# Strassen's seven products for the gate and up projections of five of seven feature groups

## The chip, the cores and the metric

The kernel runs on one core of a Trainium2 chip. A time is the device time of one execution in microseconds (us). Engines have the profile's short names: PE is TensorE's matmul, PEld its weight load, DVE is VectorE, ACT is ScalarE, POOL is GpSimd, SP is the queue that issues most DMAs. In the profile L321 is line 321 of the kernel before.

## What is computed

Two layers, each an attention step and a feed-forward step, with a residual. The change is in the feed-forward step alone:

```python
x = x + _A_ref(_layernorm(x), wq, wk, wv, wo)
x = x + (silu(n @ w_gate) * (n @ w_up)) @ w_down      # n = _layernorm(x)
# ... and both once more; x is 2048 rows of 448, w_gate and w_up are 448 x 1792
```

## The kernel before

**Precision.** Every float32 operand of a feed-forward product is held as a high and a low part in float32r (`split`, L139 and L140, on POOL for weights; ACT makes the high part and DVE the low part of activations). A product of two is then three matmuls: high by high, high by low, low by high.

**Tiles.** The 2048 rows are four chunks `c` of 512; the 1792 features are 14 slices `fc` of 128, in seven groups of two (`FG`). The 448 inputs are three full blocks `k` of 128 partitions and a rest of 64. Activations lie transposed, in `xh` and `xl` (`self.X[c]`).

**A unit** (`unit`) is one slice by one chunk. Its matmuls use half the array's rows each, and two of them run side by side (`side_by_side`, L321): one on partitions 0 to 63, one on 64 to 127, on two different PSUM banks. Two such matmuls are called a pair here. A unit has 21 pairs of 512 columns for gate and up (11, then 10 with the banks exchanged) and 12 pairs of 448 columns for down (6 and 6). On PE the order is: gate and up 11, the first down half of the unit before, gate and up 10, the second down half of the unit before. Between two halves ACT reads one column of each bank (`between`, L328, into `seen`), so that the second half waits until the first is complete. Behind gate and up come, for each unit: ACT silu (L888), DVE product (L889), ACT high part (L890), DVE low part (L893). The down product accumulates in four banks over both slices of a group, and then goes into `xres` (`accumulate`: two tiles on DVE, L792, two copied by ACT, L795, and added by POOL, L796).

**Order.** Nothing is rescheduled: each engine runs its instructions in the order in which the program issues them (`manual_schedule`). `pend` holds the down halves and adds of the last unit, `soon` and `mid` hold steps of the layer norm of chunk 3 that are given to certain units of group 0; `turned` transposes chunk 3 on PE in the middle of the unit of chunk 2, slice 1. A chunk's loop runs inside a group's. Weights of slice `fc + 3` are loaded and split by POOL at the last chunk of slice `fc` (`weights`); the raw weights have one buffer (`wr`).

Attention comes before and after. It owns `keys`, `qts`, `qraw` and `kd`, which are idle in the feed-forward step.

Of the kernel before, what the change touches and what calls it, by code (L numbers as in the profile page):

```python
# [8 lines left out]
F32 = mybir.dt.float32  # L9
F32R = mybir.dt.float32r  # L10
# [5 lines left out]
P = 128  # L16
S = 2048
# [35 lines left out]
def forward(  # L53
# [84 lines left out]
    def split(hi, lo, raw):  # L138
        nc.gpsimd.tensor_scalar(hi, raw, 1.0, 0.0, ALU.mult, ALU.add)  # L139
        nc.gpsimd.tensor_tensor(lo, raw, hi, ALU.subtract)  # L140
# [16 lines left out]
    def weights(fc):  # L157
        fs = slice(P * fc, P * fc + P)
        r = wpool.tile([P, 4, 2, P], F32, name="wr")
        for b, src in enumerate((w_gate, w_up)):  # L160
            rows3(r[:, :, b, :], src[:, fs])
        rd = wpool.tile([P, D], F32, name="wdr")
        nc.sync.dma_start(rd, w_down[fs, :])
# [114 lines left out]
    def flipped(tiles, k, pt, copy, steps=(0, 1)):  # L278

        xh, xl, xd = tiles  # L280
        twice = xd if k == 3 else None
        if 0 in steps and twice is None:
            copy(xh[:, k, :], pt)
        elif 0 in steps:
            copy(xh[0:64, k, :], pt[0:64, :])
            copy(xd[64:128, :], pt[64:128, :])
        if 1 in steps and k < 3:
            nc.vector.tensor_tensor(xl[:, k, :], pt, xh[:, k, :], ALU.subtract)
        elif 1 in steps:
            high = xh[64:128, k, :] if twice is None else xd[64:128, :]  # L290
            nc.vector.tensor_tensor(xh[64:128, k, :], pt[64:128, :], high, ALU.subtract)

    def product_T(po, a_h, a_l, tiles):

# [21 lines left out]
    def side_by_side(lower, upper):  # L316

        assert len(lower) == len(upper)
        for two in zip(lower, upper):
            for po, (a, b), start, stop in two:  # L320
                nc.tensor.matmul(po, a, b, start=start, stop=stop, skip_group_check=True)  # L321
# [3 lines left out]
    def between(*pos):  # L325

        for i, po in enumerate(pos):
            nc.scalar.copy(seen[:, i : i + 1], po[:, 0:1])  # L328
# [416 lines left out]
                        ff.left.pop(0)()  # L745

    groups = [range(f, min(f + FG, NF)) for f in range(0, NF, FG)]

    class FeedForward:
        def __init__(self, layer):  # L750
            self.layer, self.X, self.W, self.norms = layer, {}, {}, {}
            self.pend, self.soon, self.dn, self.flip, self.mid, self.left = [], [], {}, 0, {}, []
            self.nxt = Attention(1) if layer == 0 else None

        def down(self, fs, fc, d, hh, hl):


            _, _, dh, dl = self.W[fc]
            self.flip = 1 - self.flip
            one, two = ((0, 1), (2, 3)) if self.flip else ((2, 3), (0, 1))  # L760

            def step(ts, first):
                lists = []
                for upper, half in enumerate(ts):
                    rs = slice(64 * upper, 64 * upper + 64)
                    lists.append(
                        [
                            (
                                d[t][:, 0:D],
                                (a[rs, P * t : P * t + P], b[rs, :]),  # L770
                                first and fc == fs[0] and z == 0,
                                not first and fc == fs[-1] and z == 2,
                            )
                            for t in half
                            for z, (a, b) in enumerate(((hh, dh), (hh, dl), (hl, dh)))
                        ]
                    )
                side_by_side(*lists)
                if first:
# [71 lines left out]
        def unit(self, gi, c, n):  # L851
            fs = groups[gi]
            fc = fs[n]
            w = self.W[fc]
            held, pg = zip(*(bank(LOW, True) for _ in range(2)))
            first, self.pend = self.pend, []
            if self.X[c][2] is not None:
                mid = self.mid.pop((gi, c, n), [])
                lists = [by_rows(upper, b, w, self.X[c]) for b in range(2) for upper in range(2)]
                ends = [(i == 0, False) for i in range(11)], [(False, i == 9) for i in range(10)]  # L860
                side_by_side(
                    [(pg[0], o, *e) for o, e in zip(lists[0], ends[0])],
                    [(pg[1], o, *e) for o, e in zip(lists[3], ends[0])],
                )
# [23 lines left out]
            nc.scalar.activation(by_tile(sg), in_turn(pg[0]), AF.Silu)  # L888
            nc.vector.tensor_tensor(by_tile(sg), in_turn(pg[1]), by_tile(sg), ALU.mult)  # L889
            nc.scalar.copy(hh, sg)  # L890
            for f in first[:2]:
                f()
            nc.vector.tensor_tensor(hl, sg, hh, ALU.subtract)  # L893
# [49 lines left out]
        def rest(self, xb):  # L943
# [12 lines left out]
                f()  # L956
            self.soon.append([1, lambda: [f() for f in third[5:]]])
            self.mid[0, 2, 1] = [lambda ks=ks: self.turned(3, ks) for ks in ((0, 1), (2, 3))]
            for gi, fs in enumerate(groups):
                if self.layer == 1 and fine is not None and gi in (2, 3):  # L960
                    self.verdict(gi == 3)
                    if gi == 3:
                        tc.mark_branch_hint_location("again", engines=(ET.Activation, ET.DVE, ET.Pool, ET.SP, ET.PE))
                for c in range(NC):
# [89 lines left out]
```

## Time and profile before

| | us |
|---|---|
| median of 3 runs | 1980.73 (1979.33 to 1980.74) |
| the profiled execution | 1980.02 |
| its span, first to last instruction | 1978.3 |
| PE busy in the span | 1966.2 |
| DVE, ACT, POOL busy | 814.5, 1278.1, 526.4 |

A row of a timeline gives start, duration, engine, line, operation, tiles and count, and in brackets how long the engine had been idle and what it waited for. A row of groups gives busy time and mean duration in ns of one instruction. A matmul's duration runs to the end of its pipeline, so back-to-back pairs overlap: their rate is the distance of their starts.

### The profile page before, as it was taken

The numbers are of one execution on the slowest core, as the hardware profiler recorded it, in microseconds if no ns is written. First come the engines' busy times: TensorE is split into PE (matmuls) and PEld (weight loads), VectorE is DVE, ScalarE is ACT, GpSimd is POOL, SyncE is SP. The second block draws the span as 40 slices with busy tenths as digits, with TensorE's granted clock in tenths as the row PEclk, the third lists the DMA queues.
The fourth block names the chain that finished last, engine by engine and source line by source line (L and its number), as shares of the span: only waits on it lengthen the run. The fifth ranks groups of instructions, "written<-read, shape, count | busy, mean of one in ns | idle before, by whom it ended". The sixth has DMA issues, their size and how long they took to land. (4 is left out here: it accounts for less than half of the span.)

```text
span 1978.3 us, 44658 instructions
## 1 busy us (share of the span) xinstructions
PE 1966.2 (99%) x18507; PEld 1326.6 (67%) x18507; DVE 814.5 (41%) x1413; ACT 1278.1 (65%) x2137; POOL 526.4 (27%) x570
## 2 busy tenths in 40 slices
PE   9999999999999999999999999999999999999998
PEld 7544545445468999999984444454454699988887
DVE  7444543544434222322554335445454432222323
ACT  4899898998953333333349998989989433333332
POOL 4212111132213233333341221111231133233320
PEclk9999999999999999999999999999999999999999
DMA  5101120121210011100131111102121100011102
GB/s 164 54 23 30 26 50 21 34 56 30 70 33 10 22 32 32 32 24 19 51 107 35 30 31 31 44 12 60 31 56 45 32 17 29 20 32 32 32 1 76
DMA packets 93382, 77.52 MB, mean 39 GB/s; under 512 B 23510, under 2 KB 76374, under 8 KB 93174
## 3 DMA queue, kind: packets, MB, share of 16 engines
q1 hardware_dynamic: 92886, 74.16, 13.4%
q8 instruction: 146, 2.39, 0.5%
q14 instruction: 62, 0.51, 0.1%
q10 hardware_dynamic: 288, 0.46, 0.1%
HBM read 55.06 MB, written 18.74 MB: 37 GB/s over the span
## 5 line engine op out<-in xcount | busy, mean ns | idle before, releaser
L645 PE MATMUL bank<-pt,vsb 128*32 128x512 f32 x4096 | 493.3, 598 | 0.3
L604 PE MATMUL bank<-qstack,keys 32*128 32x512 f32 x1536 | 484.6, 424 | 0.0
L604 PE MATMUL three<-qstack,keys 32*128 32x512 f32 x4608 | 460.2, 425 | 1.5 <-DVE vt L538 1.2
L604 PEld LDWEIGHTS three<-qstack,keys 32*128 32x128 f32 x4608 | 254.3, 182 | 295.3 <-ACT pt L617 181.1
L321 PE MATMUL bank<-xh,wgh 64*128 64x512 f32 x1728 | 435.7, 389 | 0.1
L611 ACT ACTIVATE pt<-three 128x1536 f32<-128x1536 f32 x256 | 372.4, 1455 | 0.6 <-ACT pt L617 0.3
L617 ACT ACTIVATE pt<-three 128x1536 f32<-128x1536 f32 x256 | 371.9, 1453 | 0.0
L321 PE MATMUL bank<-xh,wgl 64*128 64x512 f32 x1404 | 361.8, 390 | 0.0
L321 PE MATMUL bank<-xl,wgh 64*128 64x512 f32 x1296 | 326.9, 389 | 0.0
L321 PE MATMUL bank<-wdh,h 64*128 64x448 f32 x1776 | 326.5, 363 | 0.3 <-ACT h L890 0.2
L889 DVE TENSOR_TENSOR sg<-bank,sg 128x512 f32<-128x512 f32 x111 | 76.8, 692 | 493.3 <-ACT sg L888 484.1
L645 PEld LDWEIGHTS bank<-pt,vsb 128*32 128x32 f32 x4096 | 107.1, 109 | 249.8 <-issue 152.6
L613 DVE COPY raw<-bank 128x512 f32<-128x512 f32 x256 | 177.5, 693 | 226.4 <-PE bank L604 224.1
L321 PEld LDWEIGHTS bank<-xh,wgh 64*128 64x128 f32 x1728 | 256.0, 184 | 15.6 <-DVE sg L889 0.7
L796 POOL TENSOR_TENSOR xres<-stage,xres 128x448 f32<-128x448 f32 x107 | 126.5, 1204 | 490.3 <-ACT stage L795 490.3
L655 DVE TENSOR_TENSOR o<-bank,o 128x512 f32<-128x512 f32 x224 | 155.0, 692 | 240.6 <-PE bank L645 236.0
L321 PEld LDWEIGHTS bank<-wdh,h 64*128 64x128 f32 x1776 | 238.2, 184 | 12.2 <-issue 2.0
L604 PEld LDWEIGHTS bank<-qstack,keys 32*128 32x128 f32 x1536 | 243.3, 183 | 0.5 <-DVE o L655 0.3
L328 ACT COPY seen<-bank 128x1 f32<-128x1 f32 x660 | 80.7, 163 | 236.8 <-PE bank L321 234.6
L321 PEld LDWEIGHTS bank<-xh,wgl 64*128 64x128 f32 x1404 | 211.5, 184 | 12.8
L321 PE MATMUL bank<-wdl,h 64*128 64x448 f32 x888 | 212.7, 367 | 0.0
L888 ACT ACTIVATE sg<-bank 128x512 f32<-128x512 f32 x111 | 66.8, 601 | 221.1 <-PE bank L321 212.2
(136 smaller groups left out, 2265.7 us busy)
## 6 DMA issues: line engine op xcount, KB each, us to landing
o<-rd SPq DMA_DIRECT2D x32, 256.0 KB
qraw<-qd SPq DMA_DIRECT2D x128, 56.0 KB
qd<-stage SPq DMA_DIRECT2D x30, 224.0 KB
xt<-xn SPq DMA_DIRECT2D x28, 224.0 KB
wdr<-in_B_w_down_dram SPq DMA_DIRECT2D x28, 224.0 KB
xn<-xt SPq DMA_DIRECT2D x7, 768.0 KB
wr<-in_B_w_gate_dram SPq DMA_DIRECT2D x28, 192.0 KB
wr<-in_B_w_up_dram SPq DMA_DIRECT2D x28, 192.0 KB
```

What stands on the lines that cost most here:

```text
L321: nc.tensor.matmul(po, a, b, start=start, stop=stop, skip_group_check=True)
L328: nc.scalar.copy(seen[:, i : i + 1], po[:, 0:1])
L604: nc.tensor.matmul(three[:, j, :] if j < 3 else one, k[js, kp, ks], q[js, part, :], start=(z == 0), stop=(z == 2), tile_position=(32 * j, 0),)
L611: nc.scalar.activation(pt, three, AF.Exp, scale=SCALE)
L613: nc.vector.tensor_copy(raw, one)
L617: nc.scalar.activation(pt, three, AF.Exp, scale=SCALE)
L645: nc.tensor.matmul(po[32 * j : 32 * j + 32, :], vsb[:, n % NT, :], pts[n][j], start=(n == 2 * d), stop=(n > 2 * d), skip_group_check=True,)
L655: nc.vector.tensor_tensor(acc, in_turn(po), acc, ALU.add)
L796: nc.gpsimd.tensor_tensor(r, s, r, ALU.add)
L888: nc.scalar.activation(by_tile(sg), in_turn(pg[0]), AF.Silu)
L889: nc.vector.tensor_tensor(by_tile(sg), in_turn(pg[1]), by_tile(sg), ALU.mult)
```

## The change

For groups 1 to 5 (`mixed`) the units are replaced by blocks: two chunks `a` and `b` by one slice. For the first two blocks `k` of the inputs, gate and up by the two chunks is a product of 2 by 2 by 2 parts (gate/up, two halves of 256 of the inputs, two chunks). The eight products of it become seven, by Strassen's scheme in its Winograd form; the other 192 inputs stay as they were. The sums of activations (`mix`, 18 DVE instructions for two chunks, put into `keys` or into new tiles) are made once a layer and pair of chunks, the sums of weights (`sums`, six POOL instructions) once a slice.

A block has 39 pairs of 512 columns (12 in A1 to A4, 27 in S0 to S5) where two units had 42, and 24 of 448 as before. Its parts are put together by six DVE additions that read PSUM (u2, w5, u3, C12, C22, C21) and one ACT copy (s1). The down product is no longer accumulated over two slices: each block adds its result to `xres`. `ORDER` is the order of a block's run; a name without "-" is of the new block, "-" of the one before, "--" of the one before that. E and F are the two down products (chunk b, chunk a), f and g are reads by `between`, x1 to x3 are places for `mix` steps, w1 and w2 for weights.

In group 0 each unit also does up to five `mix` steps at its end. The weights of a mixed group are loaded in w2 and summed and split in w1 (`jobs`). The check of the row sums (`verdict`) moves from groups 2 and 3 of the second layer to groups 0 and 6. The second copy of the program, which runs only where that check fails, keeps units.

```diff
+    mixed = () if full else range(1, len(groups) - 1)
+    ORDER = (
+        "A1 C21- Fc2-- Fp2-- mulA- A2 fY fX Fa0-- Fa1-- A3 fZ fW Fc3-- Fp3-- A4 s1 hhA- u2 x1 E1- w1 w5 fE- u3 S0 "
+        "hlA- x2 gY E2- Ea0- Ea1- x3 Ec2- Ep2- Ec3- Ep3- w2 S1 gX S2 gZ S3 gW S4 F1- C12 C22 silB mulB fF- S5 hhB hlB F2- silA"
+    ).split()
...
+        def mix(self, p):
...
+            tt = nc.vector.tensor_tensor
+            fs = []
+            for i, *terms in ((2, b1[0], b0[0], b0[1], b1[1]), (0, b0[0], a0[0], a0[1], b0[1]), (1, b1[0], t, None, b1[1]), (3, a1[0], t, None, a1[1])):
+                fs.append(lambda x=terms[0], y=terms[1]: tt(t, x, y, ALU.subtract))
+                if terms[2] is not None:
+                    fs.append(lambda x=terms[2]: tt(t, t, x, ALU.subtract))
+                fs.append(lambda x=terms[3]: tt(t, t, x, ALU.add))
+                fs.append(lambda i=i: nc.vector.tensor_copy(hi[i], t))
+                fs.append(lambda i=i: tt(lo[i], t, hi[i], ALU.subtract))
+            return fs
+
+        def sums(self, fc, r):
+
+            raw = self.apart
+            m = [raw[:, P * i : P * i + P] for i in range(4)]
+            tt = nc.gpsimd.tensor_tensor
+            tt(m[0], r[:, 0, 1, :], r[:, 1, 1, :], ALU.add)
+            tt(m[2], r[:, 0, 0, :], r[:, 0, 1, :], ALU.subtract)
+            tt(m[1], m[0], r[:, 0, 0, :], ALU.subtract)
+            tt(m[3], r[:, 1, 0, :], m[1], ALU.subtract)
+            split(*self.S[fc % 3], raw)
+
+        def block(self, p, fc):
...
+            o["A1"] = lambda: side_by_side(p1[0], p6[1])
+            o["A2"] = lambda: side_by_side(p5[0], p7[1])
+            o["A3"] = lambda: side_by_side(p6[0], p1[1])
+            o["A4"] = lambda: side_by_side(p7[0], p5[1])
...
+            cuts = (0, 7, 8, 12, 15, 20, 27)
...
+            o["s1"] = lambda: nc.scalar.copy(s_, x)
+            o["u2"] = lambda: tt(u_, y, s_, ALU.add)
+            o["w5"] = lambda: tt(w_, z, u_, ALU.add)
+            o["u3"] = lambda: tt(v_, w, u_, ALU.add)
+            o["C12"] = lambda: tt(w_, y, w_, ALU.add)
+            o["C22"] = lambda: tt(v_, z, v_, ALU.add)
+            o["C21"] = lambda: tt(u_, w, u_, ALU.add)
+            o["silB"] = lambda: nc.scalar.activation(by_tile(s_), in_turn(w_), AF.Silu)
+            o["silA"] = lambda: nc.scalar.activation(by_tile(sg), in_turn(x), AF.Silu)
+            o["mulB"] = lambda: tt(by_tile(s_), in_turn(v_), by_tile(s_), ALU.mult)
+            o["mulA"] = lambda: tt(by_tile(sg), in_turn(u_), by_tile(sg), ALU.mult)
...
+        def blocked(self, gi):
...
+            jobs = [
+                {"w1": [lambda: part(B)] if gi > mixed[0] else [], "w2": [lambda: fetch(A + 2)]},
+                {"w1": [lambda: sums(A + 2), lambda: part(A + 2)], "w2": [lambda: fetch(A + 3)]},
+                {},
+                {"w1": [lambda: sums(A + 3)]},
+            ]
+            for j, (p, fc) in enumerate((p, fc) for p in range(2) for fc in (A, B)):
+                for n, k in (("x1", 2), ("x2", 1), ("x3", 1)):
+                    jobs[j][n] = [self.extra.pop(0) for _ in range(min(k, len(self.extra)))]
+                self.blocks.append(self.block(p, fc))
+                self.run(jobs[j])
+            if last:
+                o = self.blocks[-1]
+                self.blocks.append({})
+                f = [o.pop(k) for k in ("F1", "fF", "F2")]
+                self.run({})
...
@@ unit
-            if c == NC - 1 and fc + FG + 1 < NF:
+            for _ in range(min(5, len(self.extra))):
+                self.extra.pop(0)()
+            if c == NC - 1 and mixed and not fc:
+
+                def load():
+                    r, rd = loaded(FG + 1)
+                    self.sums(FG + 1, r)
+                    self.W[FG + 1] = parted(r, rd)
+
+                self.pend.append(load)
+            elif c == NC - 1 and not mixed and fc + FG + 1 < NF:
                 self.pend.append(lambda: self.W.__setitem__(fc + FG + 1, weights(fc + FG + 1)))
@@ rest
+                self.sums(FG, columns(FG))
+                self.extra += self.mix(0)
...
+                if gi in mixed:
+                    self.blocked(gi)
...
+                for c in range(NC) if gi not in mixed else ():
                     for n in range(len(fs)):
+                        if mixed and (gi, c, n) == (0, 3, 0):
+                            self.extra += self.mix(1)
```

More of the change, by code (lines that the diff above doesn't have):

```diff
@@ L155, in forward, with columns @@
         kd, mask = pers.tile([P, 4, P], F32R, name="kdiag"), pers.tile([P, 16, 4], F32, name="mask")
-    def weights(fc):
+    def columns(fc):
         fs = slice(P * fc, P * fc + P)
@@ L752, in __init__ @@
             self.pend, self.soon, self.dn, self.flip, self.mid, self.left = [], [], {}, 0, {}, []
+            self.blocks, self.extra = [], []
             self.nxt = Attention(1) if layer == 0 else None
-        def down(self, fs, fc, d, hh, hl):
-            _, _, dh, dl = self.W[fc]
+        def mix(self, p):
+            (ah, al, _), (bh, bl, _) = self.X[2 * p], self.X[2 * p + 1]
+            (a0, a1), (b0, b1) = ([[x[:, k, :].bitcast(F32) for x in two] for k in range(2)] for two in ((ah, al), (bh, bl)))
+            hi, lo = ([t[:, z, :] for t in self.T[p]] for z in range(2))
+            t = qraw
+            tt = nc.vector.tensor_tensor
[8 more added lines that the diff above has]
+            return fs
@@ new lines, in run, with fetch, part, sums @@
+        def run(self, extra):
+            old = self.blocks
+            for name in ORDER:
+                if name in extra:
+                    for f in extra[name]:
+                        f()
+                key = name.rstrip("-")
+                back = len(name) - len(key)
+                if back < len(old):
+                    f = old[-1 - back].get(key)
+                    if f:
+                        f()
+        def blocked(self, gi):
+            A, B = groups[gi]
+            if not self.blocks:
+                one, two, *adds = self.pend
+                self.pend = []
+                self.blocks.append({"E1": one, "E2": two, "Ea0": adds[0], "Ec2": lambda: [f() for f in adds[1:]]})
+                self.tmp = pers.tile([P, 4, 512], F32, name="xn")
+            last = gi == mixed[-1]
+            def fetch(fc):
+                self.raw = loaded(fc)
+            def part(fc):
+                self.W[fc] = parted(*self.raw)
+            def sums(fc):
+                if fc // FG in mixed:
+                    self.sums(fc, self.raw[0])
+            jobs = [
[14 more added lines that the diff above has]
+                self.run({})
+                self.pend = [lambda: (f[0](), f[1]()), f[2], o["Fa0"], lambda: [o[k]() for k in ("Fc2", "Fp2", "Fa1", "Fc3", "Fp3")]]
+                part(A + 3)
@@ L759, in down @@
+        def down(self, fs, fc, d, hh, hl, w=None):
+            dh, dl = w or self.W[fc][2:]
             self.flip = 1 - self.flip
@@ L778, in step @@
                 side_by_side(*lists)
-                if first:
+                if first and w is None:
                     between(*d)
```

91 lines of the change are left out of this document (86 added, 5 removed).

## Prediction

> **What bounds the kernel now.** I read the page first (how full each engine is), then the busy time by stretch, then the timeline of one feed-forward unit.
>
> ```profile
> span 1978.3 us, 44658 instructions
> ...
> PE 1966.2 (99%) x18507; PEld 1326.6 (67%) x18507; DVE 814.5 (41%) x1413; ACT 1278.1 (65%) x2137; POOL 526.4 (27%) x570
> ```
>
> ```profile
> 480.00:960.00 480.00, 479.89 (x4385) 415.39 (x4381) 166.18 (x268) 218.02 (x563) 148.96 (x132) 1.00 0.11 30
> ```
>
> PE is full; in the second stretch, which is the first layer's feed-forward step, it is idle for 0.11 of 480 us at a granted clock of 1.00. DVE, ACT and POOL are busy 35%, 45% and 31% there. So a matmul that goes is time gained, and every wait that PE gets is time lost. The rate of the pairs:
>
> ```profile
> 599.76 0.41 PE L321 MATMUL bank<-xh,wgh 64*128 64x512 f32 x2
> ...
> 601.83 0.40 PE L321 MATMUL bank<-xh,wgh 64*128 64x512 f32 x2
> ...
> 602.29 0.38 PE L321 MATMUL bank<-wdh,h 64*128 64x448 f32 x2
> ...
> 602.56 0.24 ACT L328 COPY seen<-bank 128x1 f32<-128x1 f32 x2 [0.96 <-PE bank L321]
> ...
> 603.52 0.41 PE L321 MATMUL bank<-xh,wgh 64*128 64x512 f32 x2
> ...
> 605.59 0.41 PE L321 MATMUL bank<-xh,wgh 64*128 64x512 f32 x2
> ...
> 606.04 0.60 ACT L888 ACTIVATE sg<-bank 128x512 f32<-128x512 f32 x1 [1.97 <-PE bank L321]
> ...
> 606.67 0.69 DVE L889 TENSOR_TENSOR sg<-bank,sg 128x512 f32<-128x512 f32 x1 [4.68 <-ACT sg L888]
> ...
> 607.40 0.62 ACT L890 CAST h<-sg 128x512 fp32r<-128x512 f32 x1 [0.76 <-DVE sg L889]
> ...
> 608.05 0.69 DVE L893 TENSOR_TENSOR h<-sg,h 128x512 fp32r<-128x512 f32 x1 [0.69 <-ACT h L890]
> ```
>
> From 599.76 to 601.83 are nine pairs, 0.230 us each; six down pairs take 1.23 us (602.29 to 603.52). The same rows give the delays of a chain: a reader starts 0.22 (silu) to 0.27 us (`seen`) after the next pair could start; from ACT to DVE or back it is 0.03 to 0.04.
>
> **What goes.** Two units have 42 pairs of 512, a block 39. There are 20 blocks a layer: 2 x 20 x 3 x 0.230 = **27.6 us** less PE work. PE's order in the changed program has these 240 matmuls less, so the change does what it says. If PE never waited, that would be 1952.4.
>
> **What each block adds.** DVE gets six additions and two more `xres` adds, ACT one copy and eight more reads or copies, POOL two adds and the sums. None of it is PE work, so it costs only where PE waits. I take 0 as the end of S4 and lay PE's order end to end: F1- to 1.23, S5 2.84, F2- 4.07, A1 4.76, A2 5.45, A3 6.14, A4 6.83, E1- 8.06, S0 9.67, E2- 10.9, S1 to S4 13.9. A matmul that had to wait starts 0.16 us after its operand: 0.05 until the weight load, 0.11 by which the first matmul is longer.
>
> ```profile
> 549.43 0.59 ACT L616 ACTIVATE pt<-bank 128x512 f32<-128x512 f32 x1
> ...
> 550.07 0.16 PEld L645 LDWEIGHTS bank<-pt,vsb 128*32 128x32 f32 x8 [0.37 <-ACT pt L616]
> ```
> ```profile
> 12.56 0.50 PE L301 MATMUL bank<-xh,wh 128*128 128x512 f32 x1 [0.34 <-ACT xh L283]
> ```
>
> The chain from 0: C12 0.22 to 0.91, silB 1.54, mulB 2.26, hhB 2.92, hlB 2.95 to 3.64, C21 from 3.56 (DVE starts the next 0.61 after the last, rows 937.76 and 938.37 below) to 4.25; A2 needs it by 4.60, slack 0.35. silA 3.06 to 3.66, A1 by 3.91. A3 needs the reads fY and fX: 4.76 + 0.27 + 0.24 = 5.27, by 5.29: no slack. u2 (behind s1) 7.7, S0 by 7.9. gZ 12.48, S4 by 12.58. So a block runs at PE's rate with 0 to 0.25 us of waits; I take 0.5 us a layer: **+1.0**.
>
> **What eats this slack: POOL and DVE hold each other up.**
>
> ```profile
> 650.20 1.07 POOL L139 TENSOR_SCALAR wgh<-wr 128x1024 fp32r<-128x1024 f32 x1
> 651.36 2.40 POOL L140 TENSOR_TENSOR wgl<-wr,wgh 128x1024 fp32r<-128x1024 f32 x1
> 653.72 0.58 POOL L139 TENSOR_SCALAR wdh<-wdr 128x448 fp32r<-128x448 f32 x1
> 654.38 1.15 POOL L140 TENSOR_TENSOR wdl<-wdr,wdh 128x448 fp32r<-128x448 f32 x1
> ```
> ```profile
> 653.32 0.69 DVE L889 TENSOR_TENSOR sg<-bank,sg 128x512 f32<-128x512 f32 x1 [4.69 <-ACT sg L888]
> 654.70 1.38 DVE L893 TENSOR_TENSOR h<-sg,h 128x512 fp32r<-128x512 f32 x1 [0.69 <-ACT h L890]
> ```
> ```profile
> 937.65 2.15 POOL L140 TENSOR_TENSOR wl<-wr,wh 128x896 fp32r<-128x896 f32 x1
> 939.75 0.75 POOL L139 TENSOR_SCALAR wh<-wr 128x128 fp32r<-128x128 f32 x1
> ```
> ```profile
> 937.76 0.69 DVE L889 TENSOR_TENSOR sg<-bank,sg 128x512 f32<-128x512 f32 x1 [4.29 <-ACT sg L888]
> 938.37 0.61 DVE L792 TENSOR_TENSOR xres<-bank,xres 128x448 f32<-128x448 f32 x1
> 939.14 1.20 DVE L893 TENSOR_TENSOR h<-sg,h 128x512 fp32r<-128x512 f32 x1 [0.16 <-ACT h L890]
> ```
>
> L889 reads PSUM and SBUF and keeps 0.69 beside POOL. L893 reads SBUF twice: begun inside a POOL instruction it ends 0.55 after that ends (655.53 to 656.08; 939.80 to 940.34), and POOL's next is late in turn (0.75). So they alternate. The additions of a block read PSUM and are safe; hlA, hlB and the `mix` steps read SBUF alone and are not. Prices:
>
> ```profile
> L796 POOL TENSOR_TENSOR xres<-stage,xres 128x448 f32<-128x448 f32 x107 | 126.5, 1204 | 490.3 <-ACT stage L795 490.3
> ...
> L795 ACT COPY stage<-bank 128x448 f32<-128x448 f32 x107 | 51.6, 532 | 1.0 <-ACT seen L328 1.0
> ...
> L140 POOL TENSOR_TENSOR onl<-o,onh 128x512 fp32r<-128x512 f32 x32 | 41.4, 1292 | 2.7
> ...
> L139 POOL TENSOR_SCALAR onh<-o 128x512 fp32r<-128x512 f32 x32 | 20.1, 630 | 2.8
> ...
> L283 DVE CAST xh<-xn 128x512 fp32r<-128x512 f32 x16 | 6.5, 404 | 0.0
> ...
> L140 POOL TENSOR_TENSOR wl<-wr,wh 128x128 fp32r<-128x128 f32 x2 | 0.9, 466 | 0.2
> ```
>
> `sums` is 4 x 0.47 + 0.63 + 1.29 and gaps, 4.1 us; `parted` is 5.3 (650.20 to 655.53).
>
> *Second run of a group.* POOL has sums and split, 9.4 us, from 7.6 on, with hlA let in once; its last split ends at 17.7, which is 3.8 of the next block. hlB (2.95) then ends at 4.4 and C21 at 5.0: A2 is 0.4 late. The adds Ep2 follow, to 5.6; Fc2 on ACT needs their buffer (two in all) and waits from 4.3 to 5.6; fY and fX stand behind it and end at 6.35; A3 starts at 6.5 instead of 5.45. **1.0 us**, for groups 2 to 4. Group 1 has other steps there (below), 0.8. Both layers: **+7.6** (0 to 1.3 each). Other runs give POOL 5.3, 4.1 or nothing, and are clear by 2.1.
>
> **Entering the blocks, per layer.** The `mix` steps have a price where POOL works beside them: 0.55 us plus the rest of a POOL instruction each.
>
> ```profile
> 615.96 0.62 DVE L792 TENSOR_TENSOR xres<-bank,xres 128x448 f32<-128x448 f32 x1
> 618.28 1.29 DVE L288 TENSOR_TENSOR xl<-bank,xh 128x512 fp32r<-128x512 f32 x2 [1.71 <-ACT xh L283]
> ...
> 638.73 0.69 DVE L889 TENSOR_TENSOR sg<-bank,sg 128x512 f32<-128x512 f32 x1 [4.69 <-ACT sg L888]
> ```
> ```profile
> 615.83 2.33 POOL L796 TENSOR_TENSOR xres<-stage,xres 128x448 f32<-128x448 f32 x2 [5.09 <-ACT stage L795]
> 633.29 2.37 POOL L796 TENSOR_TENSOR xres<-stage,xres 128x448 f32<-128x448 f32 x2 [15.13 <-ACT stage L795]
> 635.61 1.07 POOL L139 TENSOR_SCALAR wgh<-wr 128x1024 fp32r<-128x1024 f32 x1
> ```
> ```profile
> 619.42 1.09 PE L275 MATMUL bank<-ident,xn 128*128 128x128 f32 x8
> ```
>
> (a) Five steps stand between the adds at 615.96 and the low parts at 618.28. The steps of the two units before push them to 617.6; alternating with two POOL adds they end at 623.0, so the first low part ends at 623.6 instead of 618.97. PE's second transposes (619.42) need that bank: **4.1** with 0.5 from a late hl before (1.1 to 4.3).
> (b) In the last unit of group 0 five more stand between hl and u2, and S0 waits for u2. POOL then does the adds (633.29), sums and split of slice 3. The steps of the unit before end at 639.5, so L889 (638.73) is 0.7 late and A2, which takes its bank, 0.6 (in the second layer A1, 0.9). hl waits for the low sums until 642.5; then split, step, split, step: 1.06 + 0.55 + 2.40 + 0.55 + 0.57 + 0.55 + 1.15 + 0.3 + 0.7 bring the last step to 650.3 and u2 to 651.0. Gate and up end at 637.88 (638.73 less silu 0.60, 0.03 and 0.22); down 1.23, the delay 0.6, A1 to A4 2.76 and E1 1.23 behind it put S0 at 643.7, and u2 at 651.16: **7.4** (1.8 if nothing is held up).
> (c) The second run has no F to put between S4 and A1: silA is ready at 3.66, A1 could start at 1.61. **2.2.**
>
> **Leaving.** The last run has E alone. behind C21 (4.25) DVE does mulA, Fa0 and Fa1, to 6.08; E1- needs the banks that Fa1 reads, 6.08 + 0.16 against 4.07; E2- needs fE, 0.7 more. **2.9.**
>
> Both layers: (a) 8.2, A1/A2 1.5, (b) 14.8, (c) 4.4, leaving 5.8, in all 34.7.
>
> **Sum** against the profiled execution's own 1980.0 (span 1978.3 and 1.7 around it, 0.7 below the median): 1980.0 - 27.6 + 1.0 + 7.6 + 34.7 = 1995.7; I forecast **1996**. The moved `verdict`, the `qraw` memset the second load of slice 2's gate and up columns on SP (256 KB, twice) and the other weight loads (issued some 10 us before POOL needs them, as `wr` comes free) lie beside full PE work: 0; if a load came late, POOL's sums would move back by as much and with them the adds behind them.
>
> [...]
>
> **Rivals.**
> 1. *The POOL work misses the DVE steps* (faster). If POOL's sums and splits of slice 3 lie before the steps, (a) is 1.1, (b) 1.8, A1/A2 0.2, the second runs cost nothing: per layer 1.1 + 1.8 + 0.2 + 2.2 + 2.9 + 0.5 = 8.7, 17.4 in all: **1970**. It turns faster where these waits stay below 27.6 together. For it: POOL is 31% busy in this stage. Against it: in the trace the split starts right behind the adds at 635.61, and each later hl that met it was held.
> 2. *Between the two*: steps and splits meet half of the time, about 1983.
> [...]
> 4. *The block's loop has no slack* (slower). Were each of A3, S0 and S4 late by 0.15, 40 blocks would add 18: **2013**. Against it: the rows above; for it: A3 has 0.02.
>
> **Chances.** Forecast (1985 to 2004) 0.50, rival 1 0.25, rival 2 0.10, rival 3 0.08, rival 4 0.07. A run of this kernel tells some 0.2%, 4 us, from no change: faster than 1976 0.25 (rival 1), within 0.10 (rival 2), slower 0.65. The range that leaves 0.2 out: 1966 to 2010; of the forecast alone 1985 to 2004.
>
> **What would show it.** PE idle near zero inside the blocks and one block in 13.9 us; in each layer a gap of 4 us in the middle of the third chunk's second unit and one of 7 ahead of the first S0, released by u2; DVE `mix` steps of 1 to 3 us beside POOL's split; two gaps of 2 us at the start of the second and the end of the last run; one of 1 us behind each second run, released by `seen`. Steps of 0.7 us without gaps would prove the forecast wrong, as would a granted clock below 1 or a block of 14.4.

## The result, and the profile after

The changed kernel takes **2036.87 us** (median of 4 runs, 2033.64 to 2038.06) against 1980.09 for the kernel before in the same comparison: a ratio of 1.0284, 95% interval 1.0267 to 1.0302, so 57 us slower. The forecast was 1996 with a range to 2010: the sign was right, the size was not, and the time lies outside the range. The profiled execution took 2036.95.

The page of the changed kernel, its span and its first table (busy time, share of the span, instructions):

```profile
span 2035.2 us, 45408 instructions
...
PE 1980.6 (97%) x18267; PEld 1291.2 (63%) x18267; DVE 1130.9 (56%) x1805; ACT 1371.1 (67%) x2417; POOL 729.2 (36%) x772
```

These two lines already split the miss. PE has 240 matmuls less, as forecast. Its idle time is 2035.2 - 1980.6 = 54.6 us, where it was 12.1: **42.5 more**, and the forecast had 43.3 (34.7 + 7.6 + 1.0). But its busy time, which should have fallen by 27.6, rose by 14.4. So the waits came to the forecast sum, though not in each part (below), and **42 us are lost where the profile calls PE busy**. Two things can do that: pairs that run at a lower rate, and short waits that the overlap of two matmuls hides (in the trace of before a pair's row lasts 0.41 us and the next starts 0.23 after it).

First the idle part: the long waits of PE in the first layer, from its timeline (in brackets the idle time and its releaser):

```profile
621.99 1.97 PE L285 MATMUL bank<-ident,xn 128*128 128x128 f32 x8 [2.76 <-DVE xl L298]
...
653.89 0.79 PE L335 MATMUL bank<-xh,kdiag 64*128 64x512 f32 x1 [6.22 <-DVE xn L851]
...
667.46 0.76 PE L335 MATMUL bank<-xh,wgh 64*128 64x512 f32 x1 [3.36 <-ACT sg L858]
...
803.07 0.50 PE L335 MATMUL bank<-xh,wgh 64*128 64x512 f32 x1 [0.91 <-ACT sg L858]
...
953.43 0.74 PE L335 MATMUL bank<-wdh,h 64*128 64x448 f32 x2 [3.28 <-ACT h L864]
956.38 0.74 PE L335 MATMUL bank<-wdh,h 64*128 64x448 f32 x2 [0.33 <-ACT seen L342]
...
985.48 0.46 PE L335 MATMUL bank<-wdh,h 64*128 64x448 f32 x1 [1.43 <-ACT stage L988]
```

In this order: the flip (the second transposes of chunk 3, (a) in the prediction), the first u2 (L851, in (b)), the fill (A1 of the second run, (c)), one of three second runs, the leaving (the last run), and one that was not forecast. The second layer has 2.76, 5.54, 2.71, three of 0.90 to 0.92, and 3.29. The flip, u2, the fill and the leaving stand where the prediction put them. The wait of the second runs does not: the prediction had it at A3, released by `seen` and caused by hlB held up; here it is at A1, released by silA. DVE's and POOL's rows show what was late there:

```profile
800.03 1.84 DVE L859 TENSOR_TENSOR xn<-xn 128x512 f32<-128x512 f32 x1 [0.60 <-ACT seen L342]
```
```profile
799.83 1.16 POOL L140 TENSOR_TENSOR wdl<-wdr,wdh 128x448 fp32r<-128x448 f32 x1
```

This is mulB (L859). It reads SBUF twice, so POOL's last split, which ends at 800.99, holds it up until 801.87; in a block without POOL beside it it takes 1.08 (below). The prediction had named only hlA, hlB and the `mix` steps as readers of SBUF alone; mulA and mulB are two more.

Now the busy part. DVE's timeline of one block of the changed kernel, from u2 to the next u2, with C12 (L854), C22 (L855), mulB (L859) and mulA (L860):

```profile
717.26 0.68 DVE L851 TENSOR_TENSOR xn<-bank,xn 128x512 f32<-128x512 f32 x1
...
724.28 0.69 DVE L854 TENSOR_TENSOR xn<-bank,xn 128x512 f32<-128x512 f32 x1 [1.54 <-ACT seen L342]
724.89 0.68 DVE L855 TENSOR_TENSOR xn<-bank,xn 128x512 f32<-128x512 f32 x1
726.17 1.08 DVE L859 TENSOR_TENSOR xn<-xn 128x512 f32<-128x512 f32 x1 [0.60 <-ACT seen L342]
...
729.34 1.59 DVE L860 TENSOR_TENSOR sg<-xn,sg 128x512 f32<-128x512 f32 x1
...
731.91 0.68 DVE L851 TENSOR_TENSOR xn<-bank,xn 128x512 f32<-128x512 f32 x1
```

From 717.26 to 731.91 is **14.65 us**; the forecast had 13.9, and two units of the kernel before take 14.6 (7.29 from one silu to the next in its trace). A block in its steady state is no shorter than the two units that it replaces: all of the saving is gone there. ACT, PE and POOL in the same block, from their timelines:

```profile
725.01 1.13 ACT L857 ACTIVATE xn<-xn 128x512 f32<-128x512 f32 x1 [1.69 <-DVE xn L854]
...
726.89 0.39 PE L335 MATMUL bank<-wdh,h 64*128 64x448 f32 x2
...
727.29 0.62 ACT L864 CAST h<-xn 128x512 fp32r<-128x512 f32 x1 [0.92 <-DVE xn L859]
...
727.82 0.59 ACT L858 ACTIVATE sg<-bank 128x512 f32<-128x512 f32 x1
...
728.55 0.46 PE L335 MATMUL bank<-xh,wgh 64*128 64x512 f32 x1 [0.24 <-ACT sg L858]
...
728.91 1.17 POOL L884 TENSOR_TENSOR xres<-stage,xres 128x448 f32<-128x448 f32 x1 [3.31 <-ACT stage L877]
```

silB (L857) reads SBUF and takes 1.13; silA (L858), the same operation with a bank as its source, 0.59. silA stands behind silB, mulB and hhB in this chain, and A1 (728.55) waits for it. mulB takes 1.08 here, where POOL does nothing beside it; mulA (729.34) takes 1.59 because it begins inside POOL's add of 728.91 as well. The view of waits (total, times, longest) has this wait at A1's weight load, and that for the `xres` adds, which stand behind the long mulA:

```profile
PEld bank L335 <- ACT sg L858: 14.5, 20, 1.3
...
PEld bank L335 <- DVE xres L882: 7.4, 25, 0.3
```

Last, the clock. Three rows of the windows view of the changed kernel (behind the five engines' busy times: granted clock, DMA share, GB/s):

```profile
656.00:660.00 4.00, 4.00 (x24) 3.64 (x24) 2.45 (x5) 1.12 (x3) 0.94 (x1) 0.57 0.01 2
...
668.00:672.00 4.00, 4.00 (x22) 3.36 (x20) 2.56 (x2) 0.93 (x5) 3.92 (x3) 0.50 0.18 52
...
956.00:960.00 4.00, 3.67 (x22) 3.15 (x22) 1.25 (x2) 1.36 (x5) 1.44 (x2) 0.52 0.01 2
```

PE is full or nearly so in these windows and gets a clock of 0.50 to 0.57. They lie behind the waits of 6.2, 3.4 and 3.3 us. Over the whole run, windows of 4 us miss 23.9 us of clock in sum; those of the kernel before miss 1.3, all at its end. Part of the 23.9 falls into the idle time itself.

So there are two theories for the 42 us. **S**: silB, mulB and mulA read SBUF with a stride of four words, which the earlier kernel's silu and product did only in PSUM; they take 1.13 us (silB) and, without POOL, 1.08 (mulB) against 0.60 and 0.69 of that silu and product, and make the block's chain late. **C**: the clock drops behind the waits. The rivals: the block is held by its pairs or reads, whatever those three operations cost; and pairs are slow behind a wait for another reason than the clock.

### The profile page after: what moved, and what is told of

It is laid out like the page before. It is cut to its first block, busy times and chain, and to the rows that moved or that the text cites. A ratio compares the mean times of both kernels' runs of the same rounds, so it can differ in the third digit from the quotient of the medians.

```text
span 2035.2 us, 45408 instructions
## 1 busy us (share of the span) xinstructions
PE 1980.6 (97%) x18267; PEld 1291.2 (63%) x18267; DVE 1130.9 (56%) x1805; ACT 1371.1 (67%) x2417; POOL 729.2 (36%) x772
## 5 line engine op out<-in xcount | busy, mean ns | idle before, releaser
L335 PE MATMUL bank<-xh,wgh 64*128 64x512 f32 x1248 | 330.7, 399 | 17.5 <-ACT sg L858 16.3
L884 POOL TENSOR_TENSOR xres<-stage,xres 128x448 f32<-128x448 f32 x160 | 198.1, 1253 | 234.6 <-ACT stage L877 234.6
L335 PE MATMUL bank<-xh,wgl 64*128 64x512 f32 x924 | 265.7, 395 | 0.0
L698 POOL TENSOR_TENSOR o<-o 128x512 f32<-128x512 f32 x32 | 41.2, 1288 | 587.3 <-DMA o<-rd 546.3
L335 PE MATMUL bank<-xl,wgh 64*128 64x512 f32 x816 | 226.0, 398 | 0.0
L335 PEld LDWEIGHTS bank<-wdh,h 64*128 64x128 f32 x1776 | 196.0, 187 | 35.0 <-DVE xres L882 7.4
L335 PEld LDWEIGHTS bank<-xh,wgh 64*128 64x128 f32 x1248 | 168.0, 188 | 50.0 <-ACT sg L858 14.5
L630 ACT ACTIVATE pt<-bank 128x512 f32<-128x512 f32 x256 | 151.5, 592 | 59.5 <-PE bank L618 59.4
L335 PE MATMUL bank<-wdl,h 64*128 64x448 f32 x888 | 184.4, 371 | 0.0
L628 ACT ACTIVATE pt<-raw 128x512 f32<-128x512 f32 x256 | 159.3, 622 | 0.0
```

Source lines behind the costliest of these rows:

```text
L628: nc.scalar.activation(pt1, raw, AF.Exp, scale=SCALE)
L630: nc.scalar.activation(pt1, one, AF.Exp, scale=SCALE)
L698: nc.gpsimd.tensor_tensor(rb, oraw, rb, ALU.mult)
L884: nc.gpsimd.tensor_tensor(r, h[e, t], r, ALU.add)
```

## Experiments

**e1_tile_order: the block's temporaries in the other order.**

```diff
-            o["C12"] = lambda: tt(w_, y, w_, ALU.add)
+            o["C12"] = lambda: tt(by_tile(w_), in_turn(y), by_tile(w_), ALU.add)
...
-            o["silB"] = lambda: nc.scalar.activation(by_tile(s_), in_turn(w_), AF.Silu)
+            o["silB"] = lambda: nc.scalar.activation(s_, w_, AF.Silu)
...
-            o["mulA"] = lambda: tt(by_tile(sg), in_turn(u_), by_tile(sg), ALU.mult)
+            o["mulA"] = lambda: tt(sg, u_, sg, ALU.mult)
```

The six additions and s1 are all changed like C12, and mulB like mulA: the stride is now on the side of the banks.

> The block's temporaries are kept in the other order: DVE and ACT read the banks with the stride of four words and write SBUF contiguously, and silB, mulB and mulA read SBUF contiguously. Nothing else changes. Theory S (the strided SBUF reads of silB, 1.12 us, and of mulB, 1.09 us, push silA and A1 back and set the block at 14.66 us): silB falls to about 0.6, mulB and mulA to about 0.7 to 0.9, u2 to u2 falls to 13.9 to 14.1, and the time to about 2010 (27 us less than the changed kernel's 2036.9). Rival (the block is held by its pairs or by the reads ahead of A3, whatever these three operations take): the block stays at 14.5 or more and the time falls by 5 us at most. The four long gaps of each layer, and the clock behind them, stay as they are under both.

Measured: **2000.77 us**, ratio 1.0101 (1.0085 to 1.0118); the changed kernel's ratio less this one is 0.0183, or 36 us. The groups of DVE and ACT (count, busy time and mean ns of one, idle time before), first of the changed kernel:

```profile
L860 DVE TENSOR_TENSOR sg<-xn,sg 128x512 f32<-128x512 f32 x40 | 61.5, 1536 | 4.2
L859 DVE TENSOR_TENSOR xn<-xn 128x512 f32<-128x512 f32 x40 | 48.6, 1215 | 23.9 <-ACT seen L342 17.3 <-ACT xn L857 6.5
...
L857 ACT ACTIVATE xn<-xn 128x512 f32<-128x512 f32 x40 | 45.1, 1128 | 66.7 <-DVE xn L854 66.7
```

and of this kernel:

```profile
L859 DVE TENSOR_TENSOR xn<-xn 128x512 f32<-128x512 f32 x40 | 28.9, 722 | 4.2
L860 DVE TENSOR_TENSOR sg<-xn,sg 128x512 f32<-128x512 f32 x40 | 28.9, 722 | 4.2
L854 DVE TENSOR_TENSOR xn<-bank,xn 128x512 f32<-128x512 f32 x40 | 27.6, 691 | 75.5 <-PE bank L335 61.7 <-ACT seen L342 13.8
...
L857 ACT ACTIVATE xn<-xn 128x512 f32<-128x512 f32 x40 | 25.3, 633 | 61.6 <-DVE xn L854 61.6
```

silB falls from 1128 to 633 ns, mulB from 1215 to 722, mulA from 1536 to 722; C12 (L854), which now reads the bank with the stride, keeps its 0.69. The means of mulB and mulA hold waits for POOL too: the median of mulB is 1083 and then 693, which is the stride alone, and mulA is 1.6 in 32 of 40 blocks, each time begun inside an add of POOL's, which in e1 it precedes. And the block:

```profile
698.91 0.69 DVE L851 TENSOR_TENSOR xn<-bank,xn 128x512 f32<-128x512 f32 x1 [1.06 <-ACT xn L850]
712.89 0.69 DVE L851 TENSOR_TENSOR xn<-bank,xn 128x512 f32<-128x512 f32 x1 [1.05 <-ACT xn L850]
```

13.98 us: 0.1 above the forecast's 13.9, 0.67 below the changed kernel. PE's rows of this block, the second down half's first pair and A1:

```profile
708.52 0.54 PE L335 MATMUL bank<-wdh,h 64*128 64x448 f32 x2
...
709.75 0.39 PE L335 MATMUL bank<-xh,wgh 64*128 64x512 f32 x1
```

Here 1.23 us lie between the two, in the changed kernel 1.66 (726.89 to 728.55): 0.43 of the 0.67 is A1's wait for silA. From A1 to the next down product it is 2.84 against 2.97, from there to S0 1.23 against 1.34. Over 38 distances of two blocks 0.67 is 25 us, near the 27 that theory S had asked for; the rival's 5 is excluded. The other 11 us are in the same chain at the ends, which the expectation had left as they were: the fill's wait falls from 3.4 to 2.3 and the leaving's from 3.6 to 1.7 (the second layer's alike), 6 us together; and the clock missed in windows, part of it within these waits, falls from 23.9 to 13.5. The wait in group 6 rose, from 1.4 to 2.5.

**e2_mix_moved: the `mix` steps elsewhere, the sums of slice 3 earlier.**

```diff
-            for _ in range(min(5, len(self.extra))):
+            room = {(1, 0): 5, (1, 1): 4, (2, 1): 7, (3, 0): 5, (3, 1): 2}.get((c, n), 0)
+            for _ in range(min(room, len(self.extra))):
...
+            if mixed and (gi, c, n) == (0, 1, 0):
+                self.early = loaded(FG + 1)
+                self.sums(FG + 1, self.early[0])
```

> The sums of slice 3's weights are made three units earlier, and the mix steps of the activations are dealt to other units (5 in chunk 1's first, 4 in its second, 7 in chunk 2's second, 5 and 2 in chunk 3's), so that none stands ahead of the flip and few ahead of the first u2; in the blocks they are dealt out differently too. Theory of the prediction (steps held up by POOL make the gaps of 2.8 and 6 us at the flip and ahead of the first S0): both gaps fall below 1 us, 15 to 17 us less idle time in both layers, so about 2021 by idle time alone. With the clock theory (half rate for some us behind each long gap) some 6 to 9 us more go, to about 2013. Rival (the gaps come from something else, or move to another place): the time stays above 2030. The block stays at 14.66 us.

Measured: **2026.27**, ratio 1.0236 (1.0219 to 1.0253), 10 us less than the changed kernel, where 16 or, with the clock, 24 were expected. Both waits go: no idle time of PE over 0.2 us is put down to the flip (L298) or to u2 any more. The prediction's cause for them holds. But a new one opens a unit later:

```profile
643.75 0.73 PE L335 MATMUL bank<-keys,kdiag 64*128 64x512 f32 x4 [2.27 <-DVE sg L1082]
```

(2.96 in the second layer), because five `mix` steps in that unit now stand beside POOL's split of slice 3, as DVE's row and POOL's show:

```profile
639.36 2.77 DVE L788 TENSOR_TENSOR qraw<-qraw,xl 128x512 f32<-128x512 f32 x1
```
```profile
638.88 2.70 POOL L140 TENSOR_TENSOR wgl<-wr,wgh 128x1024 fp32r<-128x1024 f32 x1
```

A step of 0.69 takes 2.77 and ends 0.55 behind the split, the price that the prediction had read from L893; the five take 7.5 us in place of 3.2. The changed kernel has the same ahead of its first u2: a step of 2.71 at 647.57 beside a split of 2.65 at 647.08. The waits at the flip and u2 went down by 17, the new one brings 5 in the two layers and the fill 1 more, near the 10 measured; the block stayed at 14.65. So the two causes are apart.

**g1_gap_short, g5_gap_long, g5_gap_busy: the kernel before with waits put in.** Theory C by itself, without Strassen: in four units of each layer DVE copies into a bank that PE needs next, once or five times; the third kernel gives PE 34 transposes to do meanwhile.

```diff
+            if gi in (1, 2, 3, 4) and (c, n) == (1, 0):
+                for _ in range(5):
+                    nc.vector.tensor_copy(pg[0], qraw)
+                for _ in range(34):
+                    nc.tensor.transpose(pg[1][:, 0:P], ident, ident)
```

(g1: one copy, no transposes. g5_gap_long: no transposes.)

> The kernel before, with one DVE copy ahead of a matmul of the first unit of chunk 1 in groups 1 to 4 of each layer, for which PE must wait: eight short gaps of 1.5 to 2.5 us. The outputs do not change. Idle time alone: 8 times the gap seen, 12 to 20 us, granted clock 1.00 behind each. Clock theory (a gap of about 2 us and more lowers the clock): some us more than the gaps' sum, and a granted clock below 1 in the windows behind them.

> The same with five DVE copies: eight gaps of 4.5 to 5.5 us. Idle time alone: 36 to 44 us. Clock theory, as the changed kernel's trace suggests (pairs 0.42 us apart in place of 0.23 for 3.5 to 6 us behind its long gaps): 2 to 3 us more per gap, 16 to 24 us more in all, so 52 to 68 us, with a granted clock of 0.5 to 0.6 in the 4-us windows behind each gap.

> g5_gap_long with 34 transposes of the identity on PE in each gap (0.149 us each by the first 54 of the kernel before, so 5.1 us of the gap's 5.7), into a bank that the next matmuls overwrite. The eight waits for DVE stay. Clock theory: granted clock 1.00 behind them and the time falls from 2045 to the idle part alone, 1980 + 8 x 5.7 = 2026. Rival (the slow pairs behind a gap come from the restart of the pipeline or from DVE, not from idleness): about 2045 as before.

| | wait each | idle, 8 waits | time | more than before |
|---|---|---|---|---|
| g1_gap_short | 2.8 | 22.4 | 2010.68 | 30 (26.5 to 33.3) |
| g5_gap_long | 5.7 | 45.9 | 2045.08 | 64 (61.0 to 67.7) |
| g5_gap_busy | 5.7, of which 1.9 idle | 15.1 | 2032.32 | 52 (49.1 to 55.2) |

Behind a wait of g5_gap_long, PE's timeline and then the windows view:

```profile
792.82 0.79 PE L321 MATMUL bank<-xh,wgh 64*128 64x512 f32 x2 [5.75 <-DVE bank L859]
793.41 0.63 PE L321 MATMUL bank<-xl,wgh 64*128 64x512 f32 x2
...
796.40 0.63 PE L321 MATMUL bank<-xh,wgl 64*128 64x512 f32 x2
...
799.29 0.40 PE L321 MATMUL bank<-xh,wgh 64*128 64x512 f32 x2
799.52 0.40 PE L321 MATMUL bank<-xl,wgh 64*128 64x512 f32 x2
```
```profile
1740.00:1744.00 4.00, 4.00 (x22) 3.22 (x20) 0.00 (x0) 0.24 (x2) 0.00 (x0) 0.50 0.00 0
```

Pairs come every 0.43 us (793.41 to 796.40 are seven distances) and again every 0.23 from 799.29 on; a full window gets a clock of 0.50 and 22 matmuls. So a wait of 5.7 us costs (64 - 45.9) / 8 = 2.3 us more than its length, one of 2.8 us 0.9. In g5_gap_busy the same eight waits for DVE remain and cost 12 us less, because PE has something to do: the slow pairs come from idleness, not from the restart and not from DVE. The 34 transposes took 3.8 us, not 5.1, so 1.9 us of idle were left, and three of the eight waits still lowered the clock; that fits the 6 us by which 2026 is missed. The rows show that it is no fixed price:

```profile
725.41 0.50 PE L321 MATMUL bank<-xh,wgh 64*128 64x512 f32 x2 [1.90 <-DVE bank L859]
725.75 0.40 PE L321 MATMUL bank<-xl,wgh 64*128 64x512 f32 x2
...
789.77 0.67 PE L321 MATMUL bank<-xh,wgh 64*128 64x512 f32 x2 [1.88 <-DVE bank L859]
790.24 0.64 PE L321 MATMUL bank<-xl,wgh 64*128 64x512 f32 x2
```

The first wait is followed by pairs at full rate, the second, as long, by pairs at half. In g1 five of eight waits lowered the clock, in g5_gap_long all. (The profile of g1 is of its slowest execution, 2014.54; the 0.9 us come from the median, so fewer may have dropped there.) The drops in these runs have two lengths. Behind the wait above, the windows of 4 us from 788 on have a clock of 0.96, 0.50 and 0.68: 3.4 us of clock are missing, which is 6.8 us at half. Each of the eight waits of g5_gap_long gives 3.4, each of the three in g5_gap_busy 1.7, that is 3.4 us at half; of the five in g1 one gives 3.3 and four 1.7. The granted clock of the whole span agrees within its rounding: 0.986 in g5_gap_long, that is 28.6 of 2044.1 us missing, where eight drops and the 1.3 at the end make 28.5; 0.994 in g1 and 0.997 in g5_gap_busy.

**e3_both: e1 and e2 together.**

> The block's temporaries in the other order and the mix steps and sums moved, together. If the two causes add: 2036.9 less 36 less 10.6, about 1990; if one of the gains was hidden behind the other (the block's chain and the gaps overlap), 1995 or more.

Measured: **1990.36**, ratio 1.0048 (1.0034 to 1.0062). They add. What is left of PE's waits: 2.3 in chunk 3 (2.95 in the second layer), 3.2 at the fill, 1.6 at the leaving, and 2.83 in group 6, where an ACT copy waits for a buffer of POOL's, and POOL first splits the next layer's attention weights.

**e4_more_moved: two of these moved, by the program's order.**

```diff
-                if gi == len(groups) - 2 and self.nxt:
-                    self.nxt.w = load_wqkv(xb.enter_context(tc.tile_pool(name="wqkv1", bufs=1, reuse_waits="tile")), None)[1]
...
+                        if gi == len(groups) - 1 and (c, n) == (0, 0) and self.nxt:
+                            self.nxt.w = load_wqkv(xb.enter_context(tc.tile_pool(name="wqkv1", bufs=1, reuse_waits="tile")), None)[1]
...
-                {"w1": [lambda: part(B)] if gi > mixed[0] else [], "w2": [lambda: fetch(A + 2)]},
+                {"w1": [lambda: part(B)], "w2": [lambda: fetch(A + 2)]},
```

The units of group 0 got one `mix` step more in two places (5, 5, 7, 6 and 2), the blocks two less, and the split of slice 3 at the end of group 0 went.

> The kernel of e3, and besides: POOL splits the weights of slice 3 in the first run of group 1 in place of the end of group 0, where the trace of e2 shows mix steps of 1.4 to 2.8 us beside it and a gap of 2.3 us in each layer; and the next layer's attention weights are loaded one unit later, behind the adds of the last block (in e1's trace an ACT copy waited 3.9 us for them and PE 2.5). If these are the causes, two gaps of 2.3 and one of 2.5 us go, with about 1 us of clock behind each: 7 to 10 us less than e3. If the gaps only move, within 3 us of e3.

Measured: **1990.98**, ratio 1.0054 (1.0040 to 1.0068): no gain. The wait in group 6 is gone (0.2), and the fill's fell from 3.2 to 1.9, but that in chunk 3 grew to 3.8 and 4.5, and one of 1.1 came in the second run of group 1. POOL's timeline of e4 says why:

```profile
635.09 2.81 POOL L989 TENSOR_TENSOR xres<-stage,xres 128x448 f32<-128x448 f32 x2 [13.52 <-ACT stage L988]
637.87 1.48 POOL L139 TENSOR_SCALAR wgh<-wr 128x1024 fp32r<-128x1024 f32 x1
```

The split still starts at 638 (in e3 at 637.25), beside DVE's steps, though the program now issues it a block later. In POOL's queue it stands right behind the adds of 635.09 as before; nothing that waits came between, so it starts when they end. The later place in the program moved it by 0.6 us, as nothing in POOL's queue held it there.

**e5_steps_spread: fewer steps beside POOL's split** (5, 5 and 8 in chunks 1 and 2, 3 and 3 in chunk 3; 1, 2 and 4 in a block; the load as in e4).

```diff
+            room = {(1, 0): 5, (1, 1): 5, (2, 1): 8, (3, 0): 3, (3, 1): 3}.get((c, n), 0)
...
+                for n, k in (("x1", 1), ("x2", 2), ("x3", 4)):
```

> The kernel of e3 with two edits. In e4's trace POOL's split of slice 3 still ran at the end of group 0 (POOL's queue runs ahead of the program's order), so the mix steps go where the split is not: 5, 5 and 8 in chunks 1 and 2, only 3 and 3 in chunk 3, and 1, 2 and 4 in a block. The attention weights are loaded behind the first unit of group 6, as in e4 (there that gap fell from 2.8 to 0.2 us). If the steps beside POOL's split are the cause, the gap of 2.3 to 3.0 us in chunk 3 (3.8 to 4.5 in e4, with one step more) goes in both layers, with 1 us of clock each: with the 2.8 us of the load, 8 to 11 us less than e3's 1990.4, so about 1981. If it is the number of steps in those units and not POOL, some other unit opens a gap as long and the time stays at 1987 or above.

Measured: **1984.99**, ratio 1.0025 (1.0015 to 1.0036), 5 us less than e3, half of what was expected. The wait in chunk 3 is gone in both layers. That alone does not tell POOL from the number of steps, as three steps remain in that unit, still held (1.12, 1.53 and 1.42); it is the rows of e2 that show how much POOL adds to each. The first u2 is late again (1.16 and 0.50), and the fill's wait grew from 3.2 to 5.0, as x3's four steps met POOL's adds.

**e6_all: POOL's split one run later, silA ahead of hhB in the first run, the DVE adds ahead of mulA in the last.**

```diff
-                {"w1": [lambda: sums(A + 2), lambda: part(A + 2)], "w2": [lambda: fetch(A + 3)]},
-                {},
+                {"w1": [lambda: sums(A + 2)]},
+                {"w1": [lambda: part(A + 2)], "w2": [lambda: fetch(A + 3)]},
```

> e5, and the three waits left: POOL's split of a group's next weights moves from the second run to the third, so that no run gives it 9.4 us; silA goes ahead of hhB in the first run alone, where no down product stands ahead of A1; in the last run the two adds on DVE go ahead of mulA. By the prediction's term for second runs (here 0.4 to 0.8 us in each of three or four groups a layer, by the spacing of u2 in e3), the first would give 3 to 5 us, the others 1.0 and 0.6 a layer: 6 to 9 us less than e5, about 1973, below the kernel before. If the second runs are late for another reason, the spacing of 14.4 to 14.9 stays and the gain is 2 to 4.

Measured: **1981.56**, ratio 1.0010 (1.0001 to 1.0019), 3 us less than e5. The distance of two C12 behind a second run was 14.4 in e5 and is 14.0 to 14.2 in five of six places of e6 (in all of e7): POOL's 9.4 us were the cause, as the prediction said, at 0.4 each. Six times 0.4 are 2.4 us, not the 3 to 5 expected, and the leaving gained 0.2 to 0.5 a layer (0.60 and 0.58, in the second layer 0.61 and 0.86, where e5 had 1.39 and 0.28). The fill gained 1.3 a layer and is still the longest wait: 2.67 and 1.01, in both layers. DVE's and POOL's timelines of e6 there:

```profile
648.92 1.66 DVE L791 TENSOR_TENSOR mixed<-qraw,mixed 128x512 fp32r<-128x512 f32 x1
650.61 1.54 DVE L786 TENSOR_TENSOR qraw<-xh,qraw 128x512 f32<-128x512 f32 x1
...
654.08 0.68 DVE L854 TENSOR_TENSOR xn<-bank,xn 128x512 f32<-128x512 f32 x1
```
```profile
648.87 2.73 POOL L998 TENSOR_TENSOR xres<-stage,xres 128x448 f32<-128x448 f32 x2 [5.13 <-ACT stage L997]
```

**e7_steps_early: these four steps ahead of POOL's adds.**

```diff
-                for n, k in (("x1", 1), ("x2", 2), ("x3", 4)):
+                for n, k in (("x1", 2), ("x2", 3 - j), ("x3", 1 + 2 * j)):
```

The last unit of group 0 has 2 steps in place of 3.

> e6 with the mix steps dealt out once more: 2 in place of 3 in the last unit of group 0 (in e6 u2 ended late there, gap 1.2 and 0.5 us), and in the first run 2, 3 and 1 in place of 1, 2 and 4 (in e6's trace the four stood beside POOL's adds, 0.6 to 1.7 us each, and put C12 2.5 us late: gaps of 2.7 and 1.0 us ahead of A1 and A2 in both layers). If that is their cause, the two gaps fall to about 1.2 together, 2.5 us less a layer, and 0.5 ahead of S0, with 1 to 1.5 us of clock a layer: 7 to 9 us less than e6, about 1973, below the kernel before by 0.3%. If the steps moved to the second run open a gap there, the time stays above 1978.

Measured: **1976.69** (median of 11 runs), ratio 0.9982 (0.9973 to 0.9991), 5 to 6 us less than e6 by the ratios, and not the 7 to 9 expected: this version is faster than both kernels, by 3.6 us (1.8 to 5.3) against the kernel before. Its page:

```profile
span 1975.6 us, 45364 instructions
...
PE 1951.4 (99%) x18267; PEld 1311.5 (66%) x18267; DVE 1108.4 (56%) x1805; ACT 1360.6 (69%) x2417; POOL 729.1 (37%) x772
```

PE is idle for 24.2 us, 12.1 more than in the kernel before, and its busy time is 14.8 below that kernel's. So of the 27.6 us that the seven products save, 14.8 show in PE's busy time, and its idle time takes most of these. Of the waits left, those at the fill (1.4 and 1.7 a layer) and the leaving (1.2 and 1.5) are the longest. The fill fell from 3.7 to 3.1 a layer, not to the 1.2 expected. PE's idle time is that of e6 (24.1); between the two profiled executions (1979.90 and 1977.38) the gain is in its busy time, and the windows miss 3.4 us of clock where those of e6 miss 6.8, the idle end left out of both.

## Why the prediction was wrong, step by step

- *PE bounds the kernel, 27.6 us less work.* Right: with the block at 13.98 (e1) the saving against 14.59 is 0.6 a block where 0.69 was forecast.
- *The waits at the flip, the first S0, the fill and the leaving: 34.7.* Right in place and cause, and near in sum: 2.8, 6.2, 3.4, 3.6 in the first layer and 2.8, 5.5, 2.7, 3.6 in the second make 30.6, with 0.4 ahead of A1 in the second. The flip was put too high (4.1), the fill too low (2.2): its silA was behind the long silB. e2 shows that the first two come from the steps, and the rows that POOL holds these. That all idle time (42.5 more) came so near to the forecast 43.3 is partly luck: the 34.7 and 7.6 were 31.0 and 5.4, and 1.4 in group 6 and 4.8 of short waits ahead of A1 (1.0 forecast) made up for it.
- *Second runs, +7.6.* The cause, POOL's 9.4 us, is right, by e6; the path is not: POOL held mulB and so silA and A1, not hlB and A3. The six idle times of 0.85 to 0.92 hold the block's own 0.25 too; the blocks concerned are 0.6 to 0.7 longer than their neighbours, not 1.0, and there are three a layer, not four.
- ***The block's loop runs at PE's rate, +1.0.* This step failed.** Its chain had "silB 1.54; mulB 2.26", that is 0.6 and 0.69, taken from silu and product of the kernel before. Those read banks; the block's read SBUF in steps of four words, and took 1.13 and, beside an idle POOL, 1.08. Against e1's 0.63 and 0.69 the chain came to silA 0.89 us late (0.50 by silB, 0.39 by mulB), where the slack was 0.25; and mulA, 0.9 longer by the step and by POOL's add, put the adds behind it late. The block was 0.75 longer than forecast, which over 38 distances is 29 us. Of the 0.67 that e1 took back, PE's rows put 0.43 on the wait at A1; the rest lies behind it, and how much of that is the adds was not tried apart. The prediction had a line for each of these operations in the changed code, `in_turn(w_)`, and a row of the wrong memory as its price. The traces show the price of the step: silB 1128 ns with it, 633 without (e1).
- *Rival 3, a clock that drops behind the waits, at a chance of 0.08.* The chance was the author's estimate; no row of before shows such a drop. The changed kernel's clock did drop (to 0.50 in the window from 668), behind all eight waits over 2.5 us, and behind that of 1.4. By the g kernels' prices the waits of 5.5 and 6.2 cost 2.3 each and the shorter six 0.9, in all some 10; the 42 us less 24 for the loop (29, of which 4.8 show as idle times ahead of A1) leave 18 for the clock and the rest. The windows of the changed kernel give 17 for the clock as an estimate (in each the clock missing, times PE's busy share): four of its nine drops were the long kind, 6.8 us at half. The term belonged in the sum, not among the rivals: nothing in the trace of before stood against it, as PE is idle for 0.11 of 480 us in that stage and so has no such wait.
- *Rival 4, no slack in the loop, 18 us.* The size was nearer to what came, but the places were A1 and the down product that waits for the adds, not A3, S0 and S4.
- *The other edits at nothing.* Nearly: the adds of the last block met the load of the attention weights (1.4 us in the first layer).
- *What would prove the forecast wrong* was named: "a granted clock below 1 or a block of 14.4". Both came.

With the loop's term at 29 and the clock's at 10 to 18, the prediction's own sum gives 1995.7 - 1.0 + 29 + 10 to 18 = 2034 to 2042; its other waits were some 6 too high, and 2036.87 was measured.

## What to carry to other kernels

An operation's duration is taken from a row with the same engine, the same memory and the same step through it; that the shape is the same does not do (silB took 1128 ns where silA, with the same shape, took 592 from a bank). Where a change takes a little work from PE, which here never waited, each wait that it brings can cost the slow clock behind it besides its length (0.9 us more for each wait of 2.8, 2.3 for each of 5.7), so the ends of a pipeline (fill, leaving, a step that another engine holds up) have to be priced with that. And work is moved past a busy engine by what its own queue waits for, not by its place in the program: the split that e4 issued a block later started 0.6 us later.

## What the runs showed of the hardware that was not expected

- For 128x512, a step of four float32 words costs 1.6 to 1.8 times the time where SBUF is read (ACT 1128 ns against 633; DVE, with one of two operands so, 1083 against 693 by the medians of mulB) and nothing where PSUM is read (C12 in e1 691, in the changed kernel 692).
- Waits of 1.9 us lowered PE's clock (pairs 0.43 us apart in place of 0.23) in three places of eight, of 2.8 us in five, of 5.7 us in eight (in the profiled executions); the clock stayed at half for 3.4 or for 6.8 us, the wait's end included.
- 34 transposes in the wait of 5.7 us kept the clock behind five of eight and gave back 12 of 64 us, without making any wait for DVE shorter.
